# Transposes ahead of the weighted sums, and early v through SyncE: a change to beacon attention followed by a low-rank mixer

## The chip, the cores and the metric

The kernel runs on one core of a Trainium2 chip. Five engines run their own instruction streams: PE (TensorE, matrix products), DVE (VectorE), ACT (ScalarE), POOL (GpSimd) and SP (SyncE, which here only issues DMAs). PE writes into PSUM, which this kernel uses as eight buffers of one bank each. The metric is the time on the device in microseconds (us), as the median of the runs; lower is better.

## The reference, cut to what matters

```python
# B, H, S, Nb, D = 8, 8, 576, 16, 64
k_all = concatenate([beacon_k, k], axis=2)         # 592 keys: 16 beacons, then the tokens
v_all = concatenate([beacon_v, v], axis=2)
scores = (1 / sqrt(D)) * matmul(q, k_all^T)        # causal over the tokens; beacons always seen
a = softmax(scores)
attn = matmul(a, v_all)                            # [B, H, S, D]
x = attn.transpose(0, 2, 1, 3).reshape(B, S, 512)
h = x.transpose(0, 2, 1) @ U @ V                   # U: 576 x 32, V: 32 x 576
u = x + h.transpose(0, 2, 1)
out = u + maximum(u @ w_ch1, 0) @ w_ch2            # w_ch1: 512 x 2048, w_ch2: 2048 x 512
```

All inputs are float32; the kernel computes the products in 16 bits and gives float32.

## The kernel before, in words

**Units.** Attention goes by pairs of heads: pair p is batch p // 4, heads 2c and 2c + 1 with c = p % 4. A batch has eight heads, called in halves (`HALVES`, four heads each) and in sets (`SETS`, two heads each). The 592 keys make five chunks of up to 128. For a pair the work is:

- `group_first` (batch 0) or `regroup_of` (later): copies of the loaded q and k into 16-bit tiles, `pr` for the main 512 tokens (L244) and `st` for the first 80 rows (L555).
- `qkT_units`: PE transposes q and k into PSUM tiles `tps` (L253, L255), and copies bring them to `qT` and `kT` (L256, L257). After pair 0 these copies are all on DVE.
- `score_units`: scores into PSUM tiles `sps` (L291) in two visits, groups 0 and 1 first and groups 2 and 3 second, each followed by exponentials on ScalarE (L297, four per visit, eight per pair). In the early pairs (p below 5) the mask is added by small matmuls ahead of the scores (L283).
- `av_unit`: the weighted sums of one head, PE into `po` (L315, 15 matmuls), then the reciprocal and the scaling on DVE (`rec`, L323, and `xb`, L324).

A pair's turn in the first loop, over p = 0 to 7, is called a slot here. It holds the second visit of pair p + 1, the weighted sums of pair p, the regrouping and transposes of pair p + 2, and the first visit of pair p + 2. Every PSUM tile comes from one pool of eight buffers, taken in the order in which the program asks; a slot asks for 12 (eight `sps`, two `tps`, two `po`).

**Mixer.** After the last pair of a batch `mix` puts the low-rank product (L344, L350, L376, L388) and the sum with x (L355) into a queue, and `feed` adds the units of 512-row blocks: `g_unit` (L415, `gps`, with `w1`) and `c_unit` (L431, `cps`, with `w2`). `fill` takes units out of the queue between the parts of a slot; `FIRST` says how many in each slot (none in slots 0 to 3, then 7, 5, 4, 4). `keep_warm` (L235) issues matmuls with no use for their result.

**Loads, and their order.** The engines' streams are in the order of the program text.

- Batch 0's q and k come as float32 by SyncE and ScalarE (`load_first`; tiles `stm` for the main part and `sth` for the first rows) and are rounded by the `group_first` copies.
- moe_U and moe_V come as float32 by SyncE (`small_loads`, L144 to L150, tile `small`; moe_V four times, once for each block of 32 partitions) and are rounded on GpSimd (`cast_small`, L154, L155, L158).
- Everything else is loaded by GpSimd, in DMAs that round to 16 bits on the way: v (`v_tokens`, five DMAs, L194, and `v_beacon`, L179) into `vs`, one tile for each of two batches; q and k of the later batches into `st` (L182, L176); `w1` in four parts (L165) and `w2` in two (L171).

GpSimd's stream before the first loop: first half of v of batch 0; a `group_first` copy for k of pair 1; second half of v of batch 0; the copy for pair 2; k of the first half of batch 1; the copy for pair 3; q of that half; the first part of `w1`; `cast_small`; first half of v of batch 1; k and q of the second half of batch 1; the second part of `w1`; second half of v of batch 1; the rest of `w1`; `w2`. In the loop, slot 4 adds the loads of batch 2.

From batch 2 on other loops take over, which the change does not touch.

The slot's order, which the change edits, as it stands:

```python
seq = [masks]
if p + 1 < NP1:
    seq.insert(0, sc[1])
    masks = sc[2]
...
seq += av[0:1] + qk + av[1:2]
```

Of the kernel before, what the change touches and what calls it, by code (L numbers as in the profile page):

```python
# [11 lines left out]
F32 = mybir.dt.float32  # L12
# [6 lines left out]
P = 128  # L19
# [11 lines left out]
def kernel(  # L31
# [13 lines left out]
    nc = tc.nc  # L45
# [94 lines left out]
    def small_loads():  # L140
# [7 lines left out]
        nc.sync.dma_start(out=uf[:NL, NT - 1, :], in_=moe_U[QM:S, :])  # L148
        for cc in range(NCC):
            nc.sync.dma_start(out=vf[ds(R * cc, R), :], in_=moe_V)  # L150

# [34 lines left out]

    def v_beacon(bsrc, vs):
        beacon_load(nc.gpsimd, bsrc, by_head(vs)[:, 0, :, 0:D], ALLH)

    def v_tokens(src, vs, hs):  # L190
        dst = by_head(vs)[:, :, hs, 0:D]
        for j in range(NT):
            a = Nb if j == 0 else 0
            nc.gpsimd.dma_start(  # L194
                out=dst[a : a + nq[j], j, :, :], in_=src[hs, ds(q0[j], nq[j]), :].rearrange("h p d -> p h d")
            )

    def v_loads(src, bsrc, vs):
        v_beacon(bsrc, vs)
        v_tokens(src, vs, ALLH)  # L200

# [21 lines left out]
    def emit_loads(b, L, vs):  # L223
        k_loads(b, L, ALLH)
        q_loads(b, L, ALLH)
        beacon_load(nc.gpsimd, beacon_k[b], L[0][0], ALLH)
        v_loads(v[b], beacon_v[b], vs)

# [255 lines left out]
    def load_batch(b):  # L484
        if b < DT0:
            Ls[b] = qk_tiles()
            emit_loads(b, Ls[b], vss[b % 2])
        else:
            v_loads(v[b], beacon_v[b], vss[b % 2])

# [31 lines left out]
    def load_first():  # L522

        main = gtp.tile([P, 2, H, 4 * D], F32, name="stm", tag="gT")
        head = gtp.tile([P, 2, H, D], F32, name="sth", tag="gT")
        raw["head"] = head
        Ls[0] = qk_tiles()[0], [main[:, i, :, :] for i in range(2)]

# [7 lines left out]

        kload(SETS[0])
        qload(nc.scalar, SETS[0])
        beacon_load(nc.scalar, beacon_k[0], head[:, 0, :, :], ALLH)

        nc.scalar.activation(out=warm, in_=ones, func=AF.Exp)
        for hs in SETS[1:]:
            kload(hs)
            qload(nc.sync, hs)
# [103 lines left out]
    with tc.manual_schedule(engines={ENG.PE, ENG.Activation, ENG.DVE, ENG.SP, ENG.Pool}):  # L648
        load_first()
        build_masks()  # L650
        v_beacon(beacon_v[0], vss[0])
        v_tokens(v[0], vss[0], HALVES[0])
        cast_small = small_loads()
        for i in range(NE):

# [13 lines left out]
        group_first(1, 1, V)  # L669
        v_tokens(v[0], vss[0], HALVES[1])  # L670
        for u in qkT_of(1):
            u()
        sc = scores_of(1)
        sc[0](IDLE[2])
        group_first(2, 0, G)

        Ls[1] = qk_tiles()
        k_loads(1, Ls[1], HALVES[0])
        beacon_load(nc.gpsimd, beacon_k[1], Ls[1][0][0], ALLH)
        group_first(3, 0, G)  # L680
# [183 lines left out]
```

## Time and profile before

| what | value |
|---|---|
| median of 3 runs | 364.61 us (364.49 to 365.14) |
| profiled execution | 363.8 us, span of its trace 362.0 us |
| mean granted clock of TensorE | 0.994 |
| PE busy | 350.3 us, 97% of the span |
| DVE, ACT, POOL busy | 186.1, 165.7, 103.6 us |
| PE busy from 0 to 36 us | 30.37 of 36 us |
| PE busy from 36 us on | 319.90 of 326 us |
| GpSimd's DMAs (queue 0) | 91376 packets, 64.3% of 16 engines' span |
| SyncE's and ScalarE's DMAs (queue 1) | 58704 packets, 31.9% |

The span is from the first to the last instruction of the profiled execution; its time holds 1.8 us more. A row of the timeline gives the start and the duration in us, the engine, the line of the kernel, the operation, what is written and read, how many such instructions follow one another, and in brackets how long the engine had been idle and who ended that. A row of the waits gives the total in us, the number of waits and the longest. In the chain each row is what the next one waited for.

### The profile page before, as it was taken

Reading aid. Unit: us, or ns where it says so; the run is one execution under the profiler, and the core shown is the slowest. Engines: PE = TensorE matmul, PEld = TensorE weight load, DVE = VectorE, ACT = ScalarE, POOL = GpSimd, SP = SyncE. Lnnn points to the kernel's source line nnn. Section 1 sums busy time; section 2 is a strip of 40 time slices with the busy share of each in tenths; the row PEclk is TensorE's granted clock in tenths of the full one; section 3 lists DMA queues with packets and bytes.
Section 4 is the critical chain, followed back from the end, with each engine's and each line's share of the span. In section 5 each row is a group of like instructions: output and inputs, shape, how many; then the busy total and the mean of one; then the engine's idle time right before and its main releaser. Section 6 shows DMA issues by size and latency. Waiting matters only on the chain.

```text
span 362.0 us, 7669 instructions
## 1 busy us (share of the span) xinstructions
PE 350.3 (97%) x3030; PEld 173.2 (48%) x3030; DVE 186.1 (51%) x495; ACT 165.7 (46%) x356; POOL 103.6 (29%) x151
## 2 busy tenths in 40 slices
PE   8997999999999999999989999999999999999995
PEld 3664555455565445444434444444454444444442
DVE  4686665377876444653455456444745423213311
ACT  4885661369645464367444554466502302401300
POOL 9977615606432729304730310000000000000000
PEclk9998999999999999999999999999999999999999
DMA  9999999997994999996999695234014313113112
GB/s 191 224 127 153 199 204 155 191 177 56 147 83 122 169 129 141 158 185 99 121 152 160 101 152 93 99 87 68 2 65 106 70 59 94 23 58 89 30 46 77
DMA packets 150714, 42.20 MB, mean 117 GB/s; under 512 B 133648, under 2 KB 145936, under 8 KB 150672
## 3 DMA queue, kind: packets, MB, share of 16 engines
q0 software_dynamic: 91376, 17.47, 64.3%
q1 hardware_dynamic: 58704, 23.84, 31.9%
q8 instruction: 25, 0.41, 0.5%
q10 hardware_dynamic: 592, 0.34, 0.3%
q14 instruction: 17, 0.14, 0.1%
HBM read 37.72 MB, written 9.44 MB: 130 GB/s over the span
## 4 chain that ended last, share of the span: by engine, by line
PE 84%; DMA 8%; SPq 3%; POOL 2%; DVE 1%; issue 0%; ACT 0%; POOLq 0%; ACTq 0%
PE gps L415 34%; PE cps L431 33%; PE po L315 7%; PE sps L291 6%; DMA stm<-in_q_dram 3%; DMA uT<-xb 2%; SPq L335 2%; DMA st<-in_q_dram 2%; PE tps L255 1%; DMA small<-in_moe_V_dram 1%; POOL vs L194 1%; PE qtp L344 1%; DVE ob L444 1%; SPq L176 1%; DVE uT L362 0%; PE ups L355 0%
## 5 line engine op out<-in xcount | busy, mean ns | idle before, releaser
L297 ACT ACTIVATE expt<-sps 128x496 f16<-128x496 f32 (+2 forms) x256 | 111.5, 536 | 62.6 <-PE sps L291 62.5
L415 PE MATMUL gps<-uT,w 128*128 128x512 f16 x576 | 136.4, 381 | 0.1
L431 PE MATMUL cps<-w,gT 128*128 128x512 f16 x576 | 134.5, 379 | 0.0
L419 ACT ACTIVATE gT<-gps 128x512 f16<-128x512 f32 x86 | 52.0, 609 | 101.1 <-PE gps L415 95.2
L431 PEld LDWEIGHTS <-gT 128*128 128x128 f16 x576 | 52.5, 98 | 61.4 <-issue 5.3
L415 PEld LDWEIGHTS <-w 128*128 128x128 f16 x576 | 52.4, 98 | 59.8 <-issue 4.5
L421 DVE TENSOR_SCALAR gT<-gps 128x512 f16<-128x512 f32 x58 | 39.8, 690 | 45.9 <-PE gps L415 43.9
L444 DVE TENSOR_TENSOR ob<-cps,ut 128x512 f32<-128x512 f32 x32 | 22.1, 689 | 53.2 <-PE cps L431 52.7
L315 PEld LDWEIGHTS <-expt 128*128 128x128 f16 (+1 forms) x960 | 36.8, 98 | 16.5 <-issue 3.0
L194 POOL DMA_DIRECT2D vs<-in_v_dram x50 | 39.6, 812 | 17.4 <-DMA st<-in_q_dram 5.1
L315 PE MATMUL po<-vs,expt 128*128 128x65 f16 (+1 forms) x960 | 40.2, 194 | 1.2 <-DVE ob L444 1.1
L291 PE MATMUL sps<-qT,kT 64*128 64x80 f16 (+4 forms) x384 | 34.3, 282 | 1.8 <-DVE kT L257 1.7
L324 DVE TENSOR_TENSOR xb<-po,rec 128x320 f16<-128x320 f32 x64 | 31.4, 491 | 2.2
L268 DVE TENSOR_TENSOR expt<-expt,bigmask 128x512 f16<-128x512 f16 x54 | 22.6, 418 | 10.9 <-ACT expt L297 10.9
L323 DVE RECIPROCAL rec<-po 128x5 f32<-128x5 f32 x64 | 12.0, 187 | 22.7 <-PE po L315 21.6
L291 PEld LDWEIGHTS <-kT 64*128 64x128 f16 x384 | 11.6, 94 | 25.1 <-issue 13.6
L179 POOL DMA_DIRECT2D vs<-in_beacon_v_dram x8 | 4.4, 550 | 55.3 <-PE po L315 53.9
L500 POOL DMA_DIRECT2D st<-in_q_dram x20 | 16.8, 870 | 3.3 <-DMA vs<-in_v_dram 3.2
L362 DVE TENSOR_TENSOR uT<-ups,uT 128x496 f16<-128x496 f32 x20 | 12.1, 667 | 9.8 <-DMA uT<-xb 8.9
L500 POOL DMA_DIRECT2D st<-in_k_dram x20 | 16.9, 875 | 0.6 <-issue 0.3
L255 PE MATMUL tps<-ident,pr 128*128 128x128 f16 x128 | 12.1, 226 | 0.0
L257 DVE COPY qT<-tps 128x512 f16<-128x512 f16 x16 | 10.9, 680 | 0.0
(78 smaller groups left out, 152.3 us busy)
## 6 DMA issues: line engine op xcount, KB each, us to landing
out_dram<-ob SPq DMA_DIRECT2D x36, 256.0 KB, 2.5
vs<-in_v_dram POOLq DMA_DIRECT2D x18, 128.0 KB, 6.7
w<-in_moe_w_ch_dram POOLq DMA_DIRECT2D x4, 512.0 KB, 7.4
w<-in_moe_w_ch_dram POOLq DMA_DIRECT2D x2, 1024.0 KB, 13.3
st<-in_k_dram POOLq DMA_DIRECT2D x12, 128.0 KB, 6.5
st<-in_q_dram POOLq DMA_DIRECT2D x12, 128.0 KB, 8.9
stm<-in_k_dram SPq DMA_DIRECT2D x4, 256.0 KB, 4.5
st<-in_k_dram POOLq DMA_DIRECT2D x2, 512.0 KB, 12.2
```

What stands on the lines that cost most here:

```text
L194: nc.gpsimd.dma_start(out=dst[a : a + nq[j], j, :, :], in_=src[hs, ds(q0[j], nq[j]), :].rearrange("h p d -> p h d"))
L268: nc.vector.tensor_tensor(out=e4, in0=e4, in1=bigmask, op=ALU.min)
L291: nc.tensor.matmul(ps[g, i][:, ds(o, w)], kT[hp, c, ds(P * ch, P)], qT[hp, c, ds(qa, w)], start=not early, stop=True, skip_group_check=early,)
L297: nc.scalar.activation(out=ex[i][:, ds(SLOT * g, gw[g])], in_=ps[g, i][:, 0 : gw[g]], func=AF.Exp, scale=scale)
L315: nc.tensor.matmul(po[:, j, :], ex[0 : nk[c], ds(blk[(c, j)], P)], vs[0 : nk[c], ds(c * H * E + h * E, E)], start=(c == 0), stop=(c == j),)
L324: nc.vector.tensor_tensor(out=xb[:, :, ds(h * D, D)], in0=po[:, :, 0:D], in1=r.broadcast_to([P, NT, D]), op=ALU.mult)
L415: nc.tensor.matmul(g[:, 0:n], w1[:, cc, ts(dc, P)], uT[:, cc, ds(t0, n)], start=(cc == 0), stop=(cc == NCC - 1))
L419: nc.scalar.activation(out=gT["t"][:, dc, 0:n], in_=g[:, 0:n], func=AF.Relu)
L421: nc.vector.tensor_scalar_max(out=gT["t"][:, dc, 0:n], in0=g[:, 0:n], scalar1=0.0)
L431: nc.tensor.matmul(ps[:m, :], gT["t"][:, dc, ds(P * i, m)], w2[:, dc, :], start=(dc == 0), stop=turned and dc == NDC - 1, skip_group_check ...
L444: nc.vector.tensor_tensor(out=ob[:m, :], in0=ps[:m, :], in1=gT["u"][:m, i, :], op=ALU.add)
L500: nc.gpsimd.dma_start(out=dst[a : m[j], j, :, :], in_=src[:, ds(q0[j], nq[j]), :].rearrange("h p d -> p h d"))
```

## The change

It has three parts.

1. In the first loop both transpose groups of pair p + 2, and the regrouping copies before them, come ahead of the masks and the two weighted sums of pair p. Before, the transposes stood between the two sums.
2. v of batch 0's second half and of both halves of batch 1 is loaded as float32 by SyncE into a part of a tile that also holds the first rows of q and k (`v_raw`: the beacons and five token loads for each half), and rounded on GpSimd into `vs` with two copies for each half (`v_round`: four chunks on 128 partitions, and the last chunk on 80). The three halves share one float32 buffer. Batch 0's first half stays with GpSimd's rounding DMAs, now with the beacons of that half alone.
3. The order of loads. At the start SyncE takes the main k of set 0, all beacons of k and then the first rows of k, and ScalarE takes q of sets 0 and 1. moe_V is one DMA whose source repeats the tensor four times. In GpSimd's stream k of batch 1's first half moves ahead of pair 2's copy and q of that half ahead of pair 3's copy; the roundings stand after `cast_small`, after the second and after the fourth part of `w1`, the last one ahead of `w2`.

```diff
-        for cc in range(NCC):
-            nc.sync.dma_start(out=vf[ds(R * cc, R), :], in_=moe_V)
+        nc.sync.dma_start(
+            out=vf, in_=moe_V.rearrange("(o r) s -> o r s", o=1).broadcast_to([NCC, R, S])
+        )
...
+    def v_loads(src, bsrc, vs, hs):
+        dst = by_head(vs)[:, :, hs, 0:D]
+        beacon_load(nc.gpsimd, bsrc, dst[:, 0, :, :], hs)
+        token_loads(nc.gpsimd, src, dst, hs)
+
+    def v_raw(b, hs):
+
+        dst = raw["v"]
+        beacon_load(nc.sync, beacon_v[b], dst[:, 0, :, :], hs)
+        token_loads(nc.sync, v[b], dst, hs)
+
+    def v_round(b, hs):
+        dst = by_head(vss[b % 2])
+        nc.gpsimd.tensor_copy(out=dst[:, 0 : NT - 1, hs, 0:D], in_=raw["v"][:, 0 : NT - 1, :, :])
+        nc.gpsimd.tensor_copy(out=dst[:NL, NT - 1, hs, 0:D], in_=raw["v"][:NL, NT - 1, :, :])
...
-        head = gtp.tile([P, 2, H, D], F32, name="sth", tag="gT")
+        rest = gtp.tile([P, 2 * H * D + NT * H // 2 * D], F32, name="sth", tag="gT")
+        head = rest[:, 0 : 2 * H * D].rearrange("p (i h d) -> p i h d", i=2, h=H)
         raw["head"] = head
+        raw["v"] = rest[:, 2 * H * D :].rearrange("p (j h d) -> p j h d", j=NT, d=D)
...
-        kload(SETS[0])
         qload(nc.scalar, SETS[0])
-        beacon_load(nc.scalar, beacon_k[0], head[:, 0, :, :], ALLH)
+        main_load(nc.sync, k[0], main[:, 0, SETS[0], :], SETS[0])
+        beacon_load(nc.sync, beacon_k[0], head[:, 0, :, :], ALLH)
+        head_load(nc.sync, k[0], head[:, 0, SETS[0], :], SETS[0], Nb)
+        qload(nc.scalar, SETS[1])
+        kload(SETS[1])
 
         nc.scalar.activation(out=warm, in_=ones, func=AF.Exp)
-        for hs in SETS[1:]:
+        for hs in SETS[2:]:
...
-        v_beacon(beacon_v[0], vss[0])
-        v_tokens(v[0], vss[0], HALVES[0])
+        v_loads(v[0], beacon_v[0], vss[0], HALVES[0])
         cast_small = small_loads()
+        v_raw(0, HALVES[1])
...
         group_first(1, 1, V)
-        v_tokens(v[0], vss[0], HALVES[1])
...
-        group_first(2, 0, G)
 
         Ls[1] = qk_tiles()
         k_loads(1, Ls[1], HALVES[0])
+        group_first(2, 0, G)
         beacon_load(nc.gpsimd, beacon_k[1], Ls[1][0][0], ALLH)
+        q_loads(1, Ls[1], HALVES[0])
         group_first(3, 0, G)
-        q_loads(1, Ls[1], HALVES[0])
         emit_w1(0)
         cast_small()
-        v_beacon(beacon_v[1], vss[1])
-        v_tokens(v[1], vss[1], HALVES[0])
+        v_round(0, HALVES[1])
+        v_raw(1, HALVES[0])
         k_loads(1, Ls[1], HALVES[1])
         q_loads(1, Ls[1], HALVES[1])
         emit_w1(1)
-        v_tokens(v[1], vss[1], HALVES[1])
+        v_round(1, HALVES[0])
+        v_raw(1, HALVES[1])
         emit_w1(2)
         emit_w1(3)
+        v_round(1, HALVES[1])
         emit_w2()
...
-            seq = [masks]
+            seq = []
+            prior = masks
             if p + 1 < NP1:
-                seq.insert(0, sc[1])
+                seq.append(sc[1])
                 masks = sc[2]
-            av, qk, sc = av_of(p), [], []
+            sc = []
             if p + 2 < NP1:
                 if p + 2 < NH2:
                     seq.append(lambda p=p: group_first(p + 2, 1, V))
                 else:
                     seq.append(lambda p=p: regroup_of(p + 2))
-                qk = [lambda i=i, p=p: qkT_of(p + 2)[i]() for i in range(2)]
-            seq += av[0:1] + qk + av[1:2]
+                seq += [lambda i=i, p=p: qkT_of(p + 2)[i]() for i in range(2)]
+            seq += [prior] + av_of(p)
```

More of the change, by code (lines that the diff above doesn't have):

```diff
@@ L185, in by_head, with token_loads @@
         return vs[:, :].rearrange("p (c h e) -> p c h e", h=H, e=E)
[L187 to L191, printed above, removed]
+    def token_loads(eng, src, dst, hs):
         for j in range(NT):
             a = Nb if j == 0 else 0
-            nc.gpsimd.dma_start(
+            eng.dma_start(
                 out=dst[a : a + nq[j], j, :, :], in_=src[hs, ds(q0[j], nq[j]), :].rearrange("h p d -> p h d")
             )
-    def v_loads(src, bsrc, vs):
-        v_beacon(bsrc, vs)
-        v_tokens(src, vs, ALLH)
+    def v_loads(src, bsrc, vs, hs):
[10 more added lines that the diff above has]
+        nc.gpsimd.tensor_copy(out=dst[:NL, NT - 1, hs, 0:D], in_=raw["v"][:NL, NT - 1, :, :])
     def by_token(t):
@@ L226, in emit_loads @@
         beacon_load(nc.gpsimd, beacon_k[b], L[0][0], ALLH)
-        v_loads(v[b], beacon_v[b], vs)
+        v_loads(v[b], beacon_v[b], vs, ALLH)
     def keep_warm(ps, n):
@@ L488, in load_batch @@
         else:
-            v_loads(v[b], beacon_v[b], vss[b % 2])
+            v_loads(v[b], beacon_v[b], vss[b % 2], ALLH)
     def load_whole(b):
```

## The prediction

> **What bounds the kernel now.** I read the page first. TensorE (PE) is busy nearly the whole span, so a microsecond gained elsewhere counts only where PE now stands still.
>
> ```profile
> ## 1 busy us (share of the span) xinstructions
> PE 350.3 (97%) x3030; PEld 173.2 (48%) x3030; DVE 186.1 (51%) x495; ACT 165.7 (46%) x356; POOL 103.6 (29%) x151
> ```
>
> Next, PE's own waits over the whole span. The first two rows are what the change can reach: one wait of 1.9 us for a q load, and five waits of 1.7 us together for the copy of kT out of PSUM.
>
> ```profile
> PE tps L253 <- DMA st<-in_q_dram: 1.9, 1, 1.9
> PE sps L291 <- DVE kT L257: 1.7, 5, 0.6
> ```
>
> Then the chain that ended last, 20 to 38 us, for the owner of the 1.9 us: GpSimd waits for moe_V, rounds it, issues six v loads of batch 1, and only then the k and q loads of the heads of pair 6; PE starts that pair's transposes when q has landed.
>
> ```profile
> 20.01 0.60 POOL Vsb L155
> ...
> 21.78 0.49 POOL vs L179
> 22.27 3.58 POOL vs L194 x5
> 25.85 0.74 POOL st L182
> ...
> 27.89 5.68 DMA st<-in_q_dram
> 33.58 0.05 issue
> 33.62 0.25 PE tps L253
> ```
>
> The windows of one microsecond show what the wait costs beyond itself: PE does nothing from 32 to 33, and then runs at half the granted clock until about 36.9 (columns: PE, PEld, DVE, ACT, POOL busy, clock, DMA share, GB/s).
>
> ```profile
> 32.00:33.00 1.00, 0.00 (x0) 0.00 (x0) 0.52 (x3) 0.80 (x3) 0.89 (x2) 1.00 1.14 159
> 34.00:35.00 1.00, 1.00 (x9) 0.74 (x8) 0.67 (x2) 0.00 (x0) 0.60 (x1) 0.50 1.69 174
> 35.00:36.00 1.00, 1.00 (x4) 0.44 (x3) 0.82 (x3) 0.00 (x0) 0.00 (x0) 0.50 2.25 153
> ```
>
> Last the timeline, ScalarE and GpSimd alone. ScalarE's eight exponentials of a slot take 3.38 us, then it idles 0.78 to 0.84 us; GpSimd's idle time ends with moe_V.
>
> ```profile
> 15.90 3.38 ACT L297 ACTIVATE expt<-sps 128x496 f16<-128x496 f32 x8 [0.84 <-PE sps L291]
> 20.07 3.38 ACT L297 ACTIVATE expt<-sps 128x496 f16<-128x496 f32 x8 [0.78 <-PE sps L291]
> ```
> ```profile
> 20.01 0.60 POOL L155 CAST Vsb<-small 128x496 f16<-128x496 f32 x1 [2.36 <-DMA small<-in_moe_V_dram]
> ```
>
> **The change, part by part.** I call T(p) the start of the first scores of pair p: 11.26, 15.43, 19.59, 23.75 and 27.92 for pairs 1 to 5, a period of 4.17 us.
>
> *The order in a slot.* No instruction is added; the two transpose groups go ahead of both weighted sums (0.47 us of PE each in the chain). Now DVE runs rec, xb (0.19 + 0.49), then the copies of qT and kT (about 0.75 each), and PE waits for the last. Moved ahead, the copies end some 0.7 us earlier, and what is left is PSUM: a slot takes 12 tiles of 8 buffers, so the first scores of a pair need the buffers of the slot's last exponentials. Those end at 15.06 (15.90 - 0.84) and the mask matmuls that follow at 15.15, while the scores wait until 15.43. The new period is 3.38 of exponentials, 0.47 from scores to ScalarE's start (15.43 to 15.90) and 0.12 for the last mask: 3.97. Bounds of this part: 0 and the 1.7 us of the wait row. DVE has 3.5 us of work per slot, so it still fits, but rec and xb now end 0.8 us into the next slot. The load order at the start (q of pair 1 issued by ScalarE, k's beacons by SyncE) gives about 0.15 of the wait before T(1), since the second transposes still wait for a PSUM buffer. So T = 11.1, 15.1, 19.0, and 23.0 if nothing else stood in the way.
>
> *The second half of v, batch 0.* Removed: five loads by GpSimd (3.58 us from 7.49). Added: six issues by SyncE behind moe_U and moe_V, and two roundings on GpSimd behind those of moe_V. moe_V becomes one DMA instead of four (issued at 12.21 to 15.18), so V's first issue stays at 12.2 and the last token load goes out at about 17.0 (each issue there waits for an earlier landing; spacing 0.65 to 1.0 us). Landing takes 3.7 (least of stm) to 6.4 us (most of small), so 20.7 to 23.4. GpSimd is free for the rounding once V has landed (17.6 at the first V load's 5.4 us) and the casts of 1.77 us are done: 19.4. Rounding: 1024 elements per partition at 630 ns per 512 (L244 on POOL) is 1.26, and the tail chunk 0.30 as L555. The end R of the rounding is 21.3 at best, 25.2 at worst (rival B); I take 22.9, from landings in the middle of the rows of moe_U and moe_V, which share that queue and time.
> Pair 2 is the first to need it: its sums could start at 19.0 + 2.2 = 21.25 and wait until R. Queued behind them on PE: the second sum, two keep-warm matmuls (0.43), the masks (0.37), the scores. T(4) = R + 1.8 = 24.7, against 23.75 before: here the gain of the order is more than spent. T(5) = 28.7.
>
> *k and q of batch 1.* The six v loads ahead of them in GpSimd's queue (4.12 us) become the two roundings (1.56). The last of the four issues starts 2.17 us after R and lands 5.7 us later (27.89 to 33.58), at R + 7.9 = 30.8; DVE regroups in 0.8: 31.6. PE gets to these transposes after T(5), 0.8 until the last xb, 2.2 of mixing (28.43 to 30.6) and 0.5 of scores: 32.2. So the 1.9 us wait goes, with 0.6 us of cover; without it a later landing costs as much as it is late. Before, one weighted sum had already been done ahead of 33.62, so 32.2 compares as 32.67: 0.95 us gained.
>
> *The clock.* From 33.62 to 37.20 PE did two transpose groups, one gps unit and one sum in 3.58 us; the same at full clock is 0.54 (twice the 0.27 at 43.46) + 0.86 + 0.47 = 1.87. Without the idle stretch 1.71 us are gained. The new wait for R is 1.65 us of idle PE at 21 to 23, close to the 1.86 that preceded the slow stretch; a slow stretch there costs between 0 and 1.7, and I take 0.6. [...]
>
> *v of batch 1.* GpSimd loses 12 loads (7.7 us) and gets four roundings (3.1 us). SyncE may overwrite the float32 buffer only after each rounding, so the loads run one after another: first half issued from R on (six at 0.6), landed at R + 8.1, rounded at R + 9.2, needed by pair 4 at R + 9.85. Bounds 0 and 1.0; I take 0.2. A rounding also holds up DVE's fast copies (the pr copy that ran beside the Vsb cast took 0.68, against a median of 0.33), at most 1.3 us each, and DVE has that room after 33 us.
> Behind the last rounding stands w2: second half issued at 36.92 + 0.89 and landed 15.3 later, at 53.1, needed by the third cps unit at 59.2. With v landing at about 41 and rounded at 42.6, w2 goes out 6 us later, but its queue is then empty of v: about 55, with need at 57.3. Price 0; then k and q of batch 2 land at about 62 instead of 60.6, and DVE has 2.5 us idle before its copy at 66.41. Each microsecond past these covers would cost one.
>
> Sum: 363.8 (the profiled execution: span 362.0 and 1.8 around it) - 0.95 - 1.71 + 0.2 + 0.6 = 361.9. The median of the runs is 0.8 above the profiled execution, so 362.7.
>
> **Rivals.** *A, all in time:* landings at the quick end, R = 21.4, no stall at pair 2 worth the name. T(4) = 23.2, transposes at 30.7 (compares as 31.2): 2.4 + 1.71 = 4.1 us gained, 359.7, or 360.5 by the median. For it: the queue of GpSimd carries less in these microseconds. Against it: small loads in SyncE's queue took 5 to 6.4 us between 10 and 15 us.
> *B, the one that ends slower:* the single moe_V load repeats its source four times as the outermost dimension; if only four DMA engines carry it, V is late, and GpSimd is stuck behind it. By the page's row of the hardware queue (23.84 MB in 31.9% of 16 engines) an engine moves 12.9 KB per us: 288 KB take 1.4 us on 16 engines, 5.6 on four. V lands at 21.8, casts end at 23.6, R = 25.2. Pair 2 idles 4 us, the slow clock comes there (1.7, as much as the removed one), and the transposes of pair 6 stand at R + 9.3 + 0.47 = 35.0, 1.35 later than 33.62: 365.2, or 366.0 by the median. It decides from R = 23.9 on if the clock drops (25.5 if not). The trace has no such load, so neither for nor against; late token loads have the same effect. [...]
> *C, no change:* R about 24, one slow stretch exchanged for another, the order's gain spent in the wait: 364.5.
>
> **How the numbers follow.** Forecast 0.50 (its own range 361.3 to 363.6), A 0.12, C 0.13, B 0.25. 0.2% is 0.73 us, about what this measurement can tell from no change. Faster 0.62, same 0.13, slower 0.25. The range goes from 360.2, below A, to B's 366.0.
>
> **What the profile would show.** Right: the q wait of PE at L253 gone and no half clock at 34 to 37; the kT waits smaller; a wait of PE's sums (L315) for GpSimd's rounding at 21 to 23; the first cps unit at about 54.3 instead of 56.1. Wrong: that wait 3 us or longer; a slow clock at 23 to 27; a new PE wait for w2 near 57 or for st near 63; the Vsb cast starting later than 20.

## The result, and the profile after

The changed kernel takes 369.41 us (median, 368.12 to 370.29) against 364.55 us for the kernel before, a ratio of 1.0131 with a 95% interval of 1.0096 to 1.0166. The forecast was 362.7 us and faster. The lines below are from the profiled execution: 368.12 us, span 366.5 us (before 363.8 and 362.0). Line numbers have moved: the weighted sums are now L324, the transposes L262 and L264, the roundings of v L208 and L209, the cast of moe_V L156.

PE is as busy as before, so the time that came to it is time in which it stands still: 366.5 - 350.1 = 16.4 us instead of 362.0 - 350.3 = 11.7.

```profile
PE 350.1 (96%) x3030; PEld 172.9 (47%) x3030; DVE 186.0 (51%) x495; ACT 165.6 (45%) x356; POOL 97.0 (26%) x141
```

PE's own waits in the same profile (total, number, longest). The 1.9 us for q of pair 6 and the 1.7 us for kT are gone; of q a wait of 0.5 us is left, which belongs to pair 4. In their place stands one wait of 5.3 us of the sums for GpSimd's rounding of v, and a new one of 1.1 us for a regrouping copy.

```profile
PE po L324 <- POOL vs L208: 5.3, 1, 5.3
...
PE tps L264 <- DVE pr L253: 1.1, 1, 1.1
...
PE tps L262 <- DMA st<-in_q_dram: 0.5, 1, 0.5
PE po L324 <- DVE expt L279: 0.5, 1, 0.5
PE po L324 <- DVE expt L277: 0.3, 1, 0.3
```

The chain that ended last, from 9 to 29 us, says whose the 5.3 us are: a v load that SyncE issued at 16.77 lands 9.16 us later, and the rounding and the sums of pair 2 follow it at once.

```profile
9.58 5.66 DMA sth<-in_q_dram
15.24 0.02 issue
15.26 1.47 SPq L191
16.73 0.04 issue
16.77 9.16 DMA sth<-in_v_dram
...
26.13 1.05 POOL vs L208
27.18 0.04 issue
27.22 1.81 PE po L324 x30
```

The timeline of GpSimd: moe_V's cast starts at 21.05 (20.01 before), then GpSimd idles 3.42 us for v, and the half is ready at 27.51.

```profile
21.05 0.60 POOL L156 CAST Vsb<-small 128x496 f16<-128x496 f32 x1 [4.13 <-DMA small<-in_moe_V_dram]
...
26.13 1.04 POOL L208 CAST vs<-sth 128x1024 f16<-128x1024 f32 x1 [3.42 <-DMA sth<-in_v_dram]
27.12 0.39 POOL L209 CAST vs<-sth 80x256 f16<-80x256 f32 x1
```

The timeline of SyncE's queue shows that the issues themselves were held up: the five token loads of this half took 7.64 us to issue, the five of the next half 2.58.

```profile
13.21 7.64 SPq L191 DMA_DIRECT2D sth<-in_v_dram x5
...
27.62 2.58 SPq L191 DMA_DIRECT2D sth<-in_v_dram x5
```

Last the windows of two microseconds (columns as before). From 22 to 26 PE does nothing, while the DMA engines move 80 and 37 GB/s, far less than the 222 of 18 to 20; then PE comes back at half the granted clock.

```profile
22.00:24.00 2.00, 0.00 (x0) 0.00 (x0) 1.19 (x3) 0.85 (x3) 0.62 (x3) 1.00 0.41 80
24.00:26.00 2.00, 0.00 (x0) 0.00 (x0) 0.00 (x0) 0.00 (x0) 0.00 (x0) 0.81 0.17 37
26.00:28.00 2.00, 0.78 (x15) 0.78 (x15) 0.00 (x0) 0.00 (x0) 1.87 (x3) 0.50 0.00 0
```

The clock stays at one half from 25.23 to 32.06, which is 6.83 us; before it was 33.49 to 36.90, 3.41 us. In the clock records of the traces the stretches are 3.413 us (before) and 6.827 us, two times that (after); a run below (a_v2) has 10.24 us, three times. A stretch of 3.413 us at half clock is called a window from here on.

Windows cut at the same work in both kernels split the loss. T(3) is the start of the first scores of pair 3, and `cps` the first matmul of the mixer's second product:

| stretch | before: length, PE busy | after: length, PE busy | longer by | of it PE idle |
|---|---|---|---|---|
| start to T(3) | 19.59, 16.70 | 18.99, 16.09 | -0.60 | +0.01 |
| T(3) to first `cps` | 36.53, 33.80 | 43.08, 34.72 | +6.55 | +5.63 |
| first `cps` to the end | 305.88, 299.78 | 304.43, 299.33 | -1.45 | -1.00 |

The loss lies between T(3) and `cps`: 5.63 us of idle PE and 0.92 us of slower work. T(4) already stands 6.47 us later than before (30.22 against 23.75), and 1.45 us are given back after the first `cps`; a wait of 1.1 us of the sums for an output copy is absent after.

### The profile page after: what moved, and what is told of

It reads as the page before. It is cut to its first block, busy times and chain, and to the rows that moved or that the text cites. A ratio compares the mean times of both kernels' runs of the same rounds, so it can differ in the third digit from the quotient of the medians.

```text
span 366.5 us, 7685 instructions
## 1 busy us (share of the span) xinstructions
PE 350.1 (96%) x3030; PEld 172.9 (47%) x3030; DVE 186.0 (51%) x495; ACT 165.6 (45%) x356; POOL 97.0 (26%) x141
## 4 chain that ended last, share of the span: by engine, by line
PE 84%; DMA 7%; DVE 4%; SPq 3%; issue 0%; ACT 0%; POOL 0%; POOLq 0%; ACTq 0%
PE gps L424 33%; PE cps L440 32%; PE po L324 7%; PE sps L300 6%; DMA sth<-in_v_dram 2%; DMA uT<-xb 2%; DMA sth<-in_q_dram 2%; PE tps L264 1%; SPq L344 1%; DMA stm<-in_q_dram 1%; PE qtp L353 1%; PE ups L364 1%; SPq L177 1%; SPq L183 1%; PE ups L385 1%; DVE ob L453 1%
## 5 line engine op out<-in xcount | busy, mean ns | idle before, releaser
L324 PEld LDWEIGHTS <-expt 128*128 128x128 f16 (+1 forms) x960 | 36.8, 99 | 20.3 <-issue 7.0
L324 PE MATMUL po<-vs,expt 128*128 128x65 f16 (+1 forms) x960 | 40.1, 195 | 6.1 <-POOL vs L208 5.3
L191 POOL DMA_DIRECT2D vs<-in_v_dram x35 | 28.8, 838 | 16.7 <-DMA w<-in_moe_w_ch_dram 8.9
L300 PEld LDWEIGHTS <-kT 64*128 64x128 f16 x384 | 11.6, 94 | 24.3 <-issue 15.1
L264 PE MATMUL tps<-ident,pr 128*128 128x128 f16 x128 | 11.6, 219 | 1.1 <-DVE pr L253 1.1
L279 DVE TENSOR_TENSOR expt<-expt,mask 80x80 f16<-80x80 f16 x54 | 11.3, 208 | 0.0
```

Source lines behind the costliest of these rows:

```text
L191: eng.dma_start(out=dst[a : a + nq[j], j, :, :], in_=src[hs, ds(q0[j], nq[j]), :].rearrange("h p d -> p h d"))
L300: nc.tensor.matmul(ps[g, i][:, ds(o, w)], kT[hp, c, ds(P * ch, P)], qT[hp, c, ds(qa, w)], start=not early, stop=True, skip_group_check=early,)
L324: nc.tensor.matmul(po[:, j, :], ex[0 : nk[c], ds(blk[(c, j)], P)], vs[0 : nk[c], ds(c * H * E + h * E, E)], start=(c == 0), stop=(c == j),)
```

## Experiments

Two things were to be told apart: whether v came late because the one moe_V load runs on few DMA engines (the theory of rival B), or because v behind batch 0's q, k, moe_U and moe_V on SyncE's queue is late in any case; and what each of the other parts does alone. Ratios are to the kernel before on the same chip, with 95% intervals. The kernel before spreads from 361.4 to 366.8 us over 31 runs on one chip, so parts worth less than some 0.3% are not settled by these numbers of runs. Much of that spread goes with the clock: 16 of the 31 runs have a mean granted clock of 0.997 or more and a median of 362.31 us, the other 15 have 0.995 or less and 364.61 us. One window of 3.413 us at half clock takes the mean of a 362 us span to 0.995, so in about half of its runs the kernel before does not lose the window that its profile shows.

### How many engines carry moe_V

moe_V again in four loads, the rest of the change kept (a_v4; then the changed kernel and this one once more, side by side on one chip: a_again, a_v4_again):

```diff
-        nc.sync.dma_start(
-            out=vf, in_=moe_V.rearrange("(o r) s -> o r s", o=1).broadcast_to([NCC, R, S])
-        )
+        for cc in range(NCC):
+            nc.sync.dma_start(out=vf[ds(R * cc, R), :], in_=moe_V)
```

> The changed kernel with moe_V in four DMAs of 32 partitions each again; all else as changed. Theory F (few engines: the one load that repeats moe_V four times is carried by four DMA engines, and the v loads behind it on SyncE's queue wait on those four): the Vsb cast on GpSimd starts at 18 to 20 instead of 21.05, the first rounding of v starts at 22 to 23.5 instead of 26.13, PE's wait of its weighted sums for that rounding falls from 5.3 us to 1.5 to 3 us, the half clock lasts one window or none instead of 25.2 to 32.1, and the time falls by 2 to 4.5 us, to 365 to 367. Theory L (late queue: any v load behind batch 0's q and k on SyncE's queue lands this late): the rounding still starts at 25.5 or later, PE's wait stays above 4.5 us, the time within 1 us of the changed kernel's 369.4.

a_v4: 366.94 us, 1.0099 (1.0063 to 1.0135). The cast of moe_V and the rounding of v come sooner, and PE's wait is about half as long. GpSimd's timeline, then PE's longest wait (this kernel's lines are one lower):

```profile
18.54 0.60 POOL L155 CAST Vsb<-small 128x496 f16<-128x496 f32 x1 [3.06 <-DMA small<-in_moe_V_dram]
...
23.05 1.04 POOL L207 CAST vs<-sth 128x1024 f16<-128x1024 f32 x1 [2.84 <-DMA sth<-in_v_dram]
```
```profile
PE po L323 <- POOL vs L207: 2.9, 1, 2.9
```

The clock drops for one window (from 23.80) instead of two.

> The changed kernel as it is, beside the other runs of this call, so that what the four DMAs of moe_V are worth is read on one chip. Expected: 1.0 to 1.7% above the kernel before.

> The changed kernel with moe_V in four DMAs, beside the changed kernel itself. By the two profiles (PE's wait for the rounding 5.3 against 2.9 us, half clock for 6.8 against 3.4 us) 2 to 4.5 us below the changed kernel; by the ratios of the two earlier groups of runs only about 1.2 us.

a_again: 368.60 us, 1.0136 (1.0095 to 1.0176). a_v4_again: 366.75 us, 1.0082 (1.0048 to 1.0115). By the medians the single load costs about 1.85 us in this kernel, though the two intervals overlap, and 0.8% remains without it. The profile of a_again has a shorter wait for v (3.0 us) although v is ready at nearly the same time (27.17), because its first scores began 2.15 us later (10.17 against 8.02); the wait is a race between the two.

moe_V in two loads, each of two copies:

```diff
+        for cc in range(2):
+            nc.sync.dma_start(
+                out=vf[ds(2 * R * cc, 2 * R), :],
+                in_=moe_V.rearrange("(o r) s -> o r s", o=1).broadcast_to([2, R, S]),
+            )
```

> The changed kernel with moe_V in two DMAs, each repeating the tensor twice along a leading dimension of two. Theory F: each is carried by two engines, in the worst case the same two, so 144 KB pass through each; the Vsb cast starts at 23 to 27, the rounding of v at 28 to 32, PE's wait is 7 us or more, the time is 2 to 5 us above the changed kernel's. Theory L: nothing depends on the leading dimension; the Vsb cast starts within 1 us of 21, PE's wait is 4.5 to 6 us, the time within 1 us of the changed kernel's.

371.73 us, 1.0223 (1.0119 to 1.0327), by its ratio the second worst of all, although the same bytes are moved. GpSimd's timeline and PE's waits:

```profile
23.96 0.60 POOL L158 CAST Vsb<-small 128x496 f16<-128x496 f32 x1 [7.96 <-DMA small<-in_moe_V_dram]
```
```profile
PE po L326 <- POOL vs L210: 4.7, 1, 4.7
PE tps L264 <- DMA st<-in_q_dram: 3.1, 1, 3.1
```

moe_V arrives 2.9 us later than with four copies, q loads of batch 1 that GpSimd issued on its own queue are late too, and the half clock lasts 10.24 us. In the packet records of the changed kernel moe_V's 128 packets of 2304 bytes run from 15.3 to 20.1 us with a mean of at most 3.8 in flight in any half microsecond; v's packets of 256 bytes behind them still have 3.4 to 3.8 in flight from 22 to 25 (means of a microsecond). With two loads of two copies at most 2.1 of moe_V's packets are in flight (a_v2), with four separate loads up to 9.4 (a_v4). Four engines with a backlog while the others are done, and in a_v2 the same two engines for both loads, would give such counts; the packet records do not say which engine carried a packet, so this was the author's reading and is not shown. The arrivals put the three forms in the same order: moe_V's cast starts at 18.54 and 19.44 us with four loads (a_v4, a_v4_again), at 21.05 and 20.05 with one load of four copies (the changed kernel, a_again), and at 23.96 with two loads of two; v is ready at 24.44 and 25.45, at 27.51 and 27.17, and at 30.41.

The single load put into the kernel before, alone:

```diff
-        for cc in range(NCC):
-            nc.sync.dma_start(out=vf[ds(R * cc, R), :], in_=moe_V)
+        nc.sync.dma_start(
+            out=vf, in_=moe_V.rearrange("(o r) s -> o r s", o=1).broadcast_to([NCC, R, S])
+        )
```

> The kernel before with only moe_V loaded by one DMA that repeats it four times. Theory F: moe_V itself lands 0.5 to 2 us later than 19.9, GpSimd's queue behind the Vsb cast moves with it, PE's wait for q of pair 6 grows from 1.9 to 2.4 to 4 us, the time grows by 0.5 to 2 us, to 365 to 366.6. Theory L: three issues fewer on SyncE, moe_V lands at or before 19.9, the time is within 0.7 us of 364.6 or shorter.

363.16 us, 1.0005 (0.9963 to 1.0048): no change. moe_V's cast starts at 20.70, 0.7 us later, and nothing of v stands behind it on SyncE's queue. In its profile q of pair 4 lands at 22.94 instead of 20.99 and PE waits 1.4 us for it, and at pair 6 it then waits only 0.4 and 0.2 us. The load was seen to cost time only in kernels that also have part 2 of the change, the two of the next section without batch 0's v on SyncE among them.

### Batch 0's second half of v by SyncE, alone

The kernel before, with this half as float32 through SyncE and rounded behind moe_V's casts; moe_V in four loads, the old order of the slots and of the first loads (the functions `v_raw` and `v_round` are those of the change):

```diff
         cast_small = small_loads()
+        v_raw(0, HALVES[1])
...
-        v_tokens(v[0], vss[0], HALVES[1])
...
         cast_small()
+        v_round(0, HALVES[1])
```

> The kernel before with only the second half of batch 0's v loaded as float32 by SyncE behind moe_U and moe_V (moe_V in four DMAs, old first loads, old slot order) and rounded on GpSimd behind the roundings of moe_V. Theory Z (this half is the part that costs: it is needed at 21 and cannot be there): the rounding ends at 23.5 to 25, PE's sums of pair 2 wait 2 to 4 us for it, and with the old order the transposes of pair 4 stand behind that wait too; pair 4's first scores at 26.5 to 28.5, the time 0.6 to 1.3% above the kernel before. Rival: alone, without the other loads in SyncE's queue and without the new order, it is in time like the other parts alone, and the time is within 0.7 us of the kernel before.

368.05 us, 1.0105 (1.0038 to 1.0172). This part alone gives most of the loss, in a kernel whose old order puts the transposes of pair 4 behind the waiting sum as well. GpSimd's timeline, PE's longest wait, and a window:

```profile
25.84 1.04 POOL L209 CAST vs<-sth 128x1024 f16<-128x1024 f32 x1 [4.60 <-DMA sth<-in_v_dram]
```
```profile
PE po L329 <- POOL vs L209: 5.5, 1, 5.5
```
```profile
24.00:26.00 2.00, 0.00 (x0) 0.00 (x0) 0.00 (x0) 0.00 (x0) 0.16 (x1) 0.50 0.08 15
```

The picture is that of the changed kernel: the half is ready at 27.22, the clock is halved from 23.67 to 30.50, T(4) is 30.74. Here moe_V did not come late (cast at 19.42), yet the last three token loads landed at 25.10 to 25.96. So the single load is not needed for v to be late. The packet records point at the loads of GpSimd that share these microseconds: from 20.5 to 23 us a mean of 16.0 packets of GpSimd's queue and 3.7 of SyncE's are in flight, where a_v4 has 0.5 and 17.3 from 20 to 22. No run isolates that.

Taken out of the changed kernel again, batch 0's v being loaded by GpSimd's rounding DMAs (a_v0pool; a_v0pool_v4 has moe_V in four loads as well; a_front has moe_V in four loads and the old order of GpSimd's stream up to the first part of `w1`):

```diff
-        v_raw(0, HALVES[1])
...
+        v_loads(v[0], beacon_v[0], vss[0], HALVES[1])
...
-        v_round(0, HALVES[1])
```

> The changed kernel, but the second half of v of batch 0 comes by GpSimd's rounding DMAs as before (at the same place in GpSimd's stream as before, with its beacons) and its rounding is gone; moe_V stays one load, batch 1's v stays on SyncE. Theory W (the loss is the wait of pair 2's sums for the rounding): PE's wait of 5.3 us for GpSimd's rounding is gone, pair 4's first scores start at 23 to 24.5 instead of 30.2, at most one window of half clock remains, k and q of pair 6 land at 29 to 31.5, the time falls by 4 to 7 us against the changed kernel, to within 1.5 us of the kernel before. Rival O (the order, and GpSimd standing behind the later roundings, cost as much by themselves): the time stays 2 us or more above the kernel before.

> The same as the run before, and moe_V in four DMAs. The Vsb cast starts at 18 to 19.5, so k and q of pair 6 are issued at 20 to 21 and land at 27 to 28.5, ahead of PE's need at about 31. Theory W: no wait of PE for q of pair 6, no half clock before 300 us, 1 to 3 us less than the kernel before. Rival O: as the run before, no better than the kernel before.

> The changed kernel with moe_V in four DMAs, the second half of v of batch 0 on GpSimd, and GpSimd's stream before the loop in the old order as far as it goes (the copy of pair 2 ahead of k of batch 1, the copy of pair 3 ahead of its q). Left of the change: the slot's order, batch 1's v through SyncE, the order at the very start. Theory W (what cost time was late data for pairs 2 to 4, by the rounding or by the copy of pair 2 behind the v loads): PE's waits for GpSimd of 2.5 to 5.3 us are gone, pair 2's first scores stand at 15 to 15.5, q of pair 6 lands at 28.5 to 30.5, and the time is 0.5 to 3 us below the kernel before. Theory O (the order and the later roundings cost by themselves): the time is 0.7 us or more above the kernel before although those waits are gone.

a_v0pool: 367.87 us, 1.0128 (1.0058 to 1.0197). a_v0pool_v4: 365.13 us, 1.0056 (1.0025 to 1.0086). a_front: 365.33 us, 1.0037 (1.0002 to 1.0072). The wait for v is gone in all three, but each has a new one. In the first two the six v loads now stand ahead of GpSimd's copy for pair 2 together with k of batch 1, and PE waits for that copy: the scores of pair 2 start at 19.64 and 19.33 instead of 15.13, and the clock halves at 15 us. The old stream of a_front removes most of that (T(2) 16.72), and then q of batch 1's first half is late (landed 24.37). PE's longest waits in a_v0pool and a_front:

```profile
PE tps L262 <- POOL st L569: 2.5, 1, 2.5
```
```profile
PE tps L261 <- DMA st<-in_q_dram: 2.1, 1, 2.1
```

So with moe_V in four loads on both sides, moving this half back brings 0.3 to 0.6% (1.0082 and 1.0099 to 1.0037 and 1.0056; the intervals overlap in part). With the single load it brings nothing (1.0131 and 1.0136 to 1.0128), against the 4 to 7 us expected: there batch 1's v stands behind that load, and batch 1's q from GpSimd's own queue lands 9.6 us after its issue, against 6.4 to 6.9 in a_v0pool_v4. None of the three is as fast as the kernel before. That a_front's last 0.4% comes from q being late with the new first loads is read from this trace and was not isolated.

### The order in the slots

The new order alone in the kernel before, and the old order in the changed kernel:

```diff
-            seq = [masks]
+            seq = []
+            prior = masks
             if p + 1 < NP1:
-                seq.insert(0, sc[1])
+                seq.append(sc[1])
...
-                qk = [lambda i=i, p=p: qkT_of(p + 2)[i]() for i in range(2)]
-            seq += av[0:1] + qk + av[1:2]
+                seq += [lambda i=i, p=p: qkT_of(p + 2)[i]() for i in range(2)]
+            seq += [prior] + av_of(p)
```

> The kernel before with only the slot's new order (transposes and their copies ahead of the weighted sums). By the prediction's step on the order the period of a slot falls from 4.17 to about 4.0 us: first scores of pair 4 at 23.1 to 23.3 instead of 23.75, PE's waits for the copy of kT (1.7 us in all) nearly gone. Theory 1 (the wall of the q load at 33.6 takes the gain back): PE's wait for q grows from 1.9 us by as much as the slots gain, the time stays within 0.7 us of 364.6. Theory 2 (the order itself costs, by later sums and PSUM buffers): the slots do not get shorter and the time grows by 0.7 us or more.

> The changed kernel with the slot's old order (one weighted sum, both transpose groups, the other sum); loads as changed. Theory P (the order hid work in the wait for the rounding): the transposes of pair 4 now stand behind the sum that waits until 27, so pair 4's first scores start 1 to 2.5 us later than 30.2 and the time grows by 0.5 to 2.5 us. Theory O (the order costs by itself, as it did alone on the kernel before, 0.5%): the time falls by 1 us or more.

b_order: 365.25 us, 1.0047 (1.0007 to 1.0088), slower. The period falls (pairs 1 to 3 at 11.51, 15.28, 19.13, a period of 3.8 instead of 4.17), but the gain is spent at T(4), which stands at 23.80 (before 23.75): q of pair 4 lands at 21.57 and PE waits 0.7 us. PE then reaches the transposes of pair 6 at 31.40 instead of 31.76, with both sums of pair 4 queued behind them, while q lands where GpSimd's stream puts it. In this profile that is 1.18 us later than before, so 0.36 us of the longer wait is the order and the rest the later q, whose loads the edit does not touch. The last rows of q landed at 34.76; the profile puts the wait down to `pr`, the copy that follows q's main part. The wait, and the instruction behind it:

```profile
PE tps L253 <- DVE pr L244: 4.2, 2, 3.4
```
```profile
34.80 0.23 PE L253 MATMUL tps<-ident,st 80*128 80x80 f16 x1 [3.40 <-DVE pr L244]
```

a_oldorder: 371.56 us, 1.0248 (1.0173 to 1.0323). With the rest of the change the old order is the worse one, by about 1.1% against the changed kernel's 1.0131 and 1.0136: the sums wait for v twice (6.2 us, and 1.8 us for batch 1's first half), and the clock drops in two places (24.33 to 31.2 and 41.4 to 44.8).

One cause of the late q in the kernel before is the place of moe_U's and moe_V's casts in GpSimd's stream. Moved behind k and q of pair 6, without and with the new order:

```diff
-        cast_small()
...
         q_loads(1, Ls[1], HALVES[1])
+        cast_small()
```

> The kernel before with only the roundings of moe_U and moe_V moved in GpSimd's stream, from ahead of the v loads of batch 1's first half to behind the k and q loads of its second half; v stays on GpSimd. Theory W (PE's 1.9 us wait and the half clock after it come from GpSimd's wait of 2.4 us for moe_V and 1.8 us of casts ahead of those loads): k and q of pair 6 are issued 4 us earlier and land at 29.5 to 30.5 instead of 33.6, the wait and the half clock go, 1.5 to 3.5 us faster than the kernel before. Rival D (the DMA engines bound these landings): they land less than 1.5 us earlier and the time is within 0.7 us of the kernel before.

> The kernel before with the roundings of moe_U and moe_V behind the loads of pair 6 and with the slot's new order. The order alone cost 0.5% because both sums of pair 4 then stood behind the q of pair 6 that landed at 34.5. With q landing near 31.5 the order is worth its shorter period: against the kernel with the moved roundings alone 0 to 1 us faster (first scores of pair 4 at 23 to 23.6, PE's wait for q at most 0.7 us). If it is 0.7 us or more slower, the order costs even where the data is there.

b_cast: 361.85 us, 0.9974 (0.9942 to 1.0007). b_cast_order: 362.34 us, 0.9975 (0.9951 to 0.9998). q lands at 31.47 and 30.80 instead of 33.58, between what the two theories expected, and neither profile has a half clock before 359 us. The order makes no difference here that these runs can tell. In its profile the shorter slots are again spent at T(4) (24.10, against 24.28 in b_cast): PE waits 1.4 us for the copy of pair 4's q, which landed at 21.87. So the order was not measured with all its data in time. In the profiles with the new order (b_cast_order, a_v4, a_front and the changed kernel) PE waits 1.1 to 1.2 us for `pr` in slot 4, where the transposes now come right behind the mixing and DVE first has its `uT` copies to do.

### The smaller parts

The new first loads alone, batch 1's v by SyncE alone, and both; and the changed kernel with moe_V in four loads and the old first loads:

```diff
-        kload(SETS[0])
         qload(nc.scalar, SETS[0])
-        beacon_load(nc.scalar, beacon_k[0], head[:, 0, :, :], ALLH)
+        main_load(nc.sync, k[0], main[:, 0, SETS[0], :], SETS[0])
+        beacon_load(nc.sync, beacon_k[0], head[:, 0, :, :], ALLH)
+        head_load(nc.sync, k[0], head[:, 0, SETS[0], :], SETS[0], Nb)
+        qload(nc.scalar, SETS[1])
+        kload(SETS[1])
...
-        v_beacon(beacon_v[1], vss[1])
-        v_tokens(v[1], vss[1], HALVES[0])
+        v_raw(1, HALVES[0])
...
-        v_tokens(v[1], vss[1], HALVES[1])
+        v_round(1, HALVES[0])
+        v_raw(1, HALVES[1])
...
+        v_round(1, HALVES[1])
```

> The kernel before with only the new order of the first loads (k of set 0, all beacons of k, then k's first rows on SyncE; q of sets 0 and 1 on ScalarE). Theory S (this order costs by itself: pair 0's first rows of k land later, pair 1's first rows of k wait for an earlier landing, and GpSimd stands behind them): the copy of k of pair 1 ends near 9.1 instead of 7.5 on GpSimd, q of the first half of batch 1 and all behind it moves by 1 to 1.6 us, the time grows by 0.7 to 2 us. Rival: the time is within 0.7 us of the kernel before, and the 2 us that were left after the other parts were undone come from batch 1's v through SyncE.

> The kernel before with only batch 1's v loaded as float32 by SyncE and rounded on GpSimd, at the places of the changed kernel. Theory R (the roundings cost by themselves: GpSimd stands 5 to 13 us behind the landings with w1 and w2 queued, and a rounding holds up DVE's copies and masks): the time is 0.7 us or more above the kernel before, although k and q of pair 6, no longer behind six v loads, land 2 to 4 us earlier than 33.6. Rival: those earlier landings remove PE's wait of 1.9 us and the half clock, and the time is 1 to 3 us below the kernel before.

> The kernel before with the two parts that cost nothing alone, the new first loads and batch 1's v through SyncE with its roundings; moe_V in four DMAs, batch 0's v on GpSimd, old slot order. If the parts add, 0.3 to 0.6% below the kernel before; if the gain of each is the same one (PE's wait for q of pair 6 and the half clock after it), 0.2 to 0.3%; if together they are late for something, at or above the kernel before.

> The changed kernel with moe_V in four DMAs and the old order of the first loads. Theory S: 0.7 to 2 us below the same kernel with the new first loads, that is 0.3 to 0.7% above the kernel before instead of 0.8 to 1.0%. Rival: no change, because pair 2's sums wait for the rounding at 24 to 25.5 whatever happens ahead of it.

| kernel | median us | ratio (95%) |
|---|---|---|
| b_start | 362.27 | 0.9978 (0.9946 to 1.0011) |
| b_v1raw | 362.46 | 0.9973 (0.9941 to 1.0005) |
| b_start_v1raw | 364.05 | 1.0007 (0.9969 to 1.0044) |
| a_v4_oldstart | 366.12 | 1.0051 (1.0023 to 1.0080) |

Each part alone is no loss, and perhaps a small gain; in b_v1raw q of pair 6 lands at 29.83, since GpSimd has fewer loads ahead of it. Together they give no gain. In the profile of both, v's loads from SyncE and GpSimd's q loads of batch 1's first half share the time from 15 to 25 us, q lands at 24.89, and T(4) is 28.23:

```profile
PE tps L267 <- DMA st<-in_q_dram: 2.7, 1, 2.7
```

a_v4_oldstart is still slower than the kernel before and waits 3.0 us for v (ready at 24.85), so the new first loads are not what makes v late. By its ratio it loses 0.3 to 0.5% less than a_v4 and a_v4_again, as theory S expected, but the intervals overlap.

### What the readings point to

If the late q is the one thing worth moving, the loads that GpSimd puts ahead of it can go behind it, with v left where it was. The kernel before, with the new slot order and this stream:

```diff
-        cast_small()
-        v_beacon(beacon_v[1], vss[1])
-        v_tokens(v[1], vss[1], HALVES[0])
         k_loads(1, Ls[1], HALVES[1])
         q_loads(1, Ls[1], HALVES[1])
+        v_beacon(beacon_v[1], vss[1])
+        v_tokens(v[1], vss[1], HALVES[0])
+        cast_small()
```

> The kernel before with the slot's new order, the k and q loads of pairs 6 and 7 ahead of the v loads of batch 1's first half in GpSimd's stream, and the roundings of moe_U and moe_V behind both; v stays on GpSimd throughout. k and q of pair 6 are issued at 17 to 20 and land at 26 to 28, v for pair 4 lands at 28 to 30, before PE needs either (about 31). Expected: no wait of PE for q or v, no half clock before 300 us, 1 to 3 us below the kernel before (0.3 to 0.8%). If the time is not below it, PE's waits of this stage do not set the end.

361.75 us, 0.9941 (0.9908 to 0.9975): faster than both kernels. It is not told apart from b_cast and b_cast_order, whose intervals overlap its own and whose first `cps` matmuls stand at 54.01 and 54.67. All its ten runs have a granted clock of 0.997 or more; against the 16 such runs of the kernel before (362.31 us) it gains 0.6 us, and the rest of its 2 us goes with the window of half clock, which no run of it loses. q's last load is issued at 20.46 (27.89 before) and lands at 27.39, the clock holds until 360 us, and the first `cps` matmul is earlier than the 56.12 of before and the 62.07 after. Its largest waits inside the first loop, then that matmul:

```profile
PE tps L253 <- DMA st<-in_q_dram: 1.1, 1, 1.1
PE tps L255 <- DVE pr L244: 1.1, 1, 1.1
```
```profile
54.54 1.04 PE L431 MATMUL cps<-w,gT 128*128 128x512 f16 x4
```

## Why the prediction was wrong

The sign was wrong, and the time is 3.4 us above the range. The step that failed is "The second half of v, batch 0": SyncE issued v's loads later, and they landed later, than the step allowed, so R was 27.51 instead of 22.9, and PE stood still for 5.3 us instead of 1.65.

| step | forecast | measured in the changed kernel |
|---|---|---|
| T(1), T(2), T(3) | 11.1, 15.1, 19.0 | 11.37, 15.13, 18.99 |
| period of the slots | 3.97 | 3.76 and 3.86; no wait for kT |
| end R of the first rounding | 22.9, bounds 21.3 to 25.2 | 27.51 |
| the two roundings | 1.26 + 0.30 | 1.04 + 0.39 |
| T(4) | R + 1.8 = 24.7 | R + 2.7 = 30.22 |
| q of pair 6 landed | R + 7.9 = 30.8 | R + 9.0 = 36.49 |
| clock | -1.71, and +0.6 for a new stretch | two windows at half clock instead of one |
| batch 1's v | +0.2 | no wait for it; 0.5 elsewhere |
| w2 | 0 | no wait, though issued 12.7 us later (a_v4_oldstart and a_v2 do wait, 1.2 and 1.4 us) |

- **Landing.** Two terms are mis-sized: "the last token load goes out at about 17.0" and "Landing takes 3.7 (least of stm) to 6.4 us (most of small)". The five token loads took 10.4, 9.8, 10.3, 9.2 and 6.5 us, and the last was issued from 19.64 to 20.86. It landed at 26.14, where the forecast had 20.7 to 23.4; for this last one the late issue is the larger part, for the four ahead of it the landing. The two prices were taken from loads that had other neighbours: the first loads of the queue. b_v0raw shows the lateness without the single load (rounding from 25.84), the pair a_again and a_v4_again that the single load adds about 1.85 us.
- **What R does to the rest.** The formula was right that everything hangs on R: T(4), the four issues of k and q, and their landing moved with it. It was short by 0.9 at T(4), because PE ran at half clock from the sums on: 1.81 us for both sums, against 1.08 at full clock.
- **The clock.** Taken as a gain of 1.71 and a chance price of 0.6. A gain was to be had only as long as no new idle stretch came, and the changed kernel has one of 5.30 us, with two windows at half clock. Removing the old wait by itself was worth 0.26% in b_cast (interval -0.58 to +0.07%), some 1 us by that ratio and less than the 0.95 + 1.71 of the sum. That average mixes two kinds of runs: beside the 17 runs that b_cast (361.85) is compared with, it is 2.3 us below the 8 with a clock of 0.995 or less (364.12) and 0.4 us below the other 9 (362.28). So the price of the old wait was nearly right for a run like the profiled one, and the forecast took it as present in every run.
- **The order.** T(1) to T(3) were right to 0.3 us. Two of its prices were missed: it brings PE sooner to whatever is late (b_order, 1.0047, where q of pair 4 takes the gain back), and `pr` in slot 4 now waits behind `uT` on DVE (1.1 us).
- **Batch 1's v.** Covered as forecast. "DVE has that room after 33 us" was not: beside the third rounding a mask of DVE at 48 us took 1.03 us, against a median of 0.19, and PE's sums waited 0.5 us for it. (The 0.3 us for another mask stand in b_order and b_best too, which round no v on GpSimd.)
- **Rival B** had the place, the order of events and the sign: a late moe_V, GpSimd stuck, the sums of pair 2 waiting, the slow clock there. That four engines carry moe_V is shown by no run; measured were at most 3.8 of its packets in flight, against up to 9.4 with four loads (a_v4). It gave 366.0 because its R of 25.2 let v land before moe_V's casts ended; moe_V was there sooner than B had it (cast at 21.05, where B had it land at 21.8), but v stood behind it and R was 2.3 later. Among what would show the forecast wrong it was said: that wait 3 us or longer, a slow clock at 23 to 27, the cast of moe_V later than 20. All three are in the profile.

The forecast weighed 0.25 for B on the ground that the trace had no such load. The trace of before did hold a warning that was used the wrong way round: the four moe_V loads took 5.0 to 6.0 us to land with less ahead of them on that queue than the token loads would have, so for the token loads these rows were no reason for the middle of the range. Nor were they a firm lower bound: in a_v4_oldstart the token loads took 4.5 to 5.9 us, and v was late there because the last of them was issued at 19.10.

## What to carry to other kernels

A load moved from an engine's queue to another is priced by what is in front of it there and by what shares the time, not by the best landings of that queue (here 3.7 us at best, and 6.5 to 10.4 for the moved loads); ask first when the data is needed, and leave the earliest-needed load where it was in time. When a profile shows one late load, look at what its issuing engine does ahead of it: putting k and q of pair 6 ahead of v and the casts, with the new order, gave 0.6%, where rerouting v lost 1.3%. An order that brings the tensor engine sooner to a late operand, with useful work queued behind, can turn a gain in period into a longer wait (b_order: a period of 3.8 instead of 4.17 us, and a wait of 3.4 instead of 1.9). And a profile is one run: look at the granted clock of the others before its waits are priced (0.997 or more in 16 of 31 runs of the kernel before, 0.994 in its profile).

## What the runs showed of the hardware

- One DMA whose source repeats moe_V four times in front delivered it later than four separate loads did, and two DMAs of two copies later still (casts at 20.05 and 21.05, 18.54 and 19.44, and 23.96 us). The loads behind suffered more than it did: in the changed kernel moe_V's cast came 1 us later than before, v up to 10.4 us after its issue. SyncE's issue of a load took up to 2.82 us there, against 0.31 to 0.69 us for the loads it issued from 7.8 to 12.7 us; a_v4, with four loads, has an issue of 2.80 us too.
- Idle stretches of PE of 1.86 us (before) and of 5.30 us (after) went with half clock for one and two windows of 3.413 us. The 3.0 us of a_again and the 2.9 us of a_v4 went with one window each, so in these profiles the slow time came in steps of 3.413 us. The length of the wait alone does not give their number: 2.54 us went with two windows in a_v0pool, 3.81 us with one in a_v4_again. Before each of the 15 drops in the first 60 us of the profiles PE had idled 1.60 us or more in the 3.413 us ahead; the waits of 1.13 to 1.45 us in b_bcast, b_best and b_cast_order went with none.
- Two of DVE's mask products took longer beside GpSimd's third rounding of v. The changed kernel has 54 of 80x80 elements; 52 of them took 0.19 us. The one beside the rounding of 128x1024 elements took 1.03 us and ended at 49.10, 0.04 us after that rounding, and the next, beside the rounding of the last chunk, took 0.38 us (DVE's timeline):

```profile
48.07 1.03 DVE L279 TENSOR_TENSOR expt<-expt,mask 80x80 f16<-80x80 f16 x1
```

The size, 0.8 us, is from this row. The mask products of 128x512 elements just ahead of each of the two (from 47.74 and 49.03) took 0.42 and 0.41 us, as everywhere else (0.41 to 0.43); no run shows what makes the difference.
